# Attention and FFN on one core: a first row turned by TensorE, loads behind the row, a last tile whole

## The chip, the cores and the metric

The kernel runs on one core of a Trainium2 chip. The metric is the device time of one execution in microseconds; for the kernel before, three runs gave 1577.24, 1580.03 and 1580.16, median 1580.03. The engines are TensorE (PE), VectorE (DVE), ScalarE (ACT), GpSimd (POOL) and SyncE (SP, which here only issues DMAs).

## The reference

Eight batches of eight heads, sequence 1152, head size 64. The queries are averaged in pairs, so 576 of them meet 1152 keys; the result feeds an FFN over 4608 tokens whose activation is h - tanh(h).

```
q_pool = q.reshape(B, H, S // factor, factor, D).mean(axis=3)
scores = scale * np.matmul(q_pool, k.transpose(0, 1, 3, 2))
scores = scores - np.max(scores, axis=-1, keepdims=True)
attn = np.exp(scores)
attn = attn / (np.sum(attn, axis=-1, keepdims=True) + 1e-09)
return np.matmul(attn, v)
...
h = x @ w_in
g = h - np.tanh(h)
return g @ w_out
```

## The kernel before

**Pairs of heads.** The attention works on 32 pairs; a pair is two heads of one batch, one on the lower and one on the upper 64 partitions. A tile `raw` (128 partitions) holds 576 columns of summed queries and 1152 columns of keys. `kq_h` is it rounded to the short float that TensorE takes at full rate, `kq_l` the rest, so that a product is three matmuls: high-high, high-low, low-high.

**A pair's course on PE.** 18 places of scores (two halves of the queries by nine key tiles). Each place has the three kinds of product and a fourth matmul, `ps<-m_row,sel`, that adds the negative row maximum from a row tile `m_row`; ScalarE then takes the exponential into `p`. Then come 18 places of p times v, and last `sums`, 24 records of `ps<-sum,ones` that add what POOL had summed over three key tiles each (`add_p`, twelve POOL additions a pair). Between a pair's score places stand the 14 `max_part` of the next pair: a product in high parts alone, and a DVE reduce into `mx`. `max_row` then makes the row: reduces into `nm`, a DVE transpose into `tr`, a DMA out to `m_dram` and one or two back into `m_row`.

**What sets the order.** Every engine runs its instructions in the order of the program, through one helper, so nearly all instructions bear its line (L37). Work beside the main course is put at a place of a pair by `add(pair, place, function)`; places 0 to 17 are scores, NS + 0 to NS + 17 (NS = 18) are p times v. SP's DMAs all go out on one queue, in order. `load(pi)` issues q and k of a pair three pairs ahead, at place 10. POOL issues two accumulating DMAs at a pair's end: `kq_l<-raw` (NS + 16) and, by `query_sums`, `raw<-in_q_dram` (NS + 17), which adds the other query of each two to the one that `load` brought. Every fourth pair ends a batch: `fetch_sums` and `reciprocals` bring the sums of its heads (`s_dram`, `rec`, `r_dram`).

**Weights.** From pair 2 on, 16 blocks of raw weights (8-byte numbers) are loaded (`w_raw`, `w_off`, 1 MB each), taken apart on ScalarE and DVE in six steps (begin, clamp, mid, high, a mask, low; four steps a pair), and stored (`wi_dram`, `wo_dram`, 512 KB twice). Late pairs also prepare the first x tile (`x_l`, `x_r`, `x_h`), and in pair 27 `first_weights` loads the first FFN weights.

**The start.** Pair 0's q comes whole, its k in three parts. Nine `max_part` give the first three query tiles, and a first `max_row` their part of the row; the other five parts and a second `max_row` follow.

**The FFN.** 9 chunks of 512 tokens by 16 feature tiles. A step is `hidden` (12 matmuls), `shrink` (ScalarE: square, two polynomials' squares, tanh; POOL: a mask; DVE: five operations and a masked copy) and `second` (12 matmuls into four `ps_o`). `g_high` and `g_low` part the result in two. Only the very last step is cut in halves of 256 tokens (`parts`): its first half gives the first two of its four output tiles, and they are stored before the second half's.

Of the kernel before, what the change touches and what calls it, by code (L numbers as in the profile page):

```python
# [6 lines left out]

F32 = mybir.dt.float32
# [4 lines left out]
ALU = mybir.AluOpType  # L13
# [33 lines left out]
def attention_ffn_kernel(  # L47
# [50 lines left out]
    chunks = [(t, 512) for t in range(0, NTOK, 512)]  # L98
    wi, wo = {}, {}

    def load_w(tile_, f, which):

        t = tile_[:, which * 1024:(which + 1) * 1024] if tile_.shape[1] == 2048 else tile_[:, 0:1024]
        sp.dma_start(t.bitcast(F32), (wi_dram, wo_dram)[which][f].rearrange("p s n -> p (s n)" if which else "p s c n -> p (s c n)"))
        if which == 0:
            wi[f] = t.rearrange("p (s c n) -> p s c n", s=2, c=NP)
        else:
            wo[f] = t.rearrange("p (s n) -> p s n", s=2)

    class X:  # L110
# [25 lines left out]
        def high(self, c):  # L136
            act.activation(self.h[:, c], self.r[c], AF.Copy)
# [27 lines left out]
    def hidden(s):  # L165

        mm = [(w, x, c) for w, x in ((0, s.x.h), (0, s.x.l), (1, s.x.h)) for c in range(NP)]
        for k in s.parts:
            for j, (w, x, c) in enumerate(mm):
                pe.matmul(s.h[:, k], wi[s.f][:, w, c], x[:, c, k], start=(j == 0), stop=(j == len(mm) - 1))  # L170

    def g_high(s, k=slice(0, 512)):
        act.activation(s.g_h[:, k], s.s1[:, k], AF.Copy)

    def g_low(s, k=slice(0, 512)):
        pool.tensor_tensor(s.g_l[:, k], s.s1[:, k], s.g_h[:, k].bitcast(F32), op=ALU.subtract)

    def shrink(s, before):
        t = lambda name, dt=F32: gp.tile([P, 512], dt, name=name)
        all_ = t("g_u"), t("g_t"), t("g_s1"), t("g_s2"), t("g_m", mybir.dt.uint8), s.w  # L180
        s.s1 = all_[2]
        s.g_h = gp.tile([P, 512], F32R, name="g_hi", bufs=LAG + 1)
        s.g_l = gp.tile([P, 512], F32R, name="g_lo", bufs=LAG + 1)
        for k in s.parts:
            shrink_part(s, before, s.h[:, k], *(a[:, k] for a in all_))
            before = None

    def shrink_part(s, before, h, u, th, s1, s2, m, w):
        act.activation(u, h, AF.Square)
        act.activation(s1, u, AF.Square, bias=pc[:, 0:1])  # L190
        act.activation(s2, u, AF.Square, bias=pc[:, 1:2])
        act.activation(th, h, AF.Tanh)
        if before:
            g_high(before)
        pool.tensor_scalar(m, u, T_POLY * T_POLY, None, op0=ALU.is_ge)
        if before:
            g_low(before)
        dve.scalar_tensor_tensor(w, u, -P0, h, op0=ALU.add, op1=ALU.mult)
        dve.scalar_tensor_tensor(w, u, PL, w, op0=ALU.mult, op1=ALU.mult)
        dve.scalar_tensor_tensor(w, s1, P1, w, op0=ALU.add, op1=ALU.mult)  # L200
        dve.scalar_tensor_tensor(s1, s2, P2, w, op0=ALU.add, op1=ALU.mult)
        dve.tensor_tensor(th, h, th, op=ALU.subtract)
        dve.copy_predicated(s1, m, th)

    def second(s, js):
        po = s.chunk.po
        for j in js:
            if len(po) <= j:
                po.append(ps_o.tile([P, DM], F32, name="ps_o"))
            ts = slice(j * P, (j + 1) * P)  # L210
            for i, (g, w) in enumerate(((s.g_h, 0), (s.g_h, 1), (s.g_l, 0))):
                pe.matmul(po[j], g[:, ts], wo[s.f][:, w], start=(s.f == 0 and i == 0), stop=(s.f == NF - 1 and i == 2))

    def store(c, j):
        o = outp[0].tile([P, DM], F32, name="o_f")
# [13 lines left out]
    with ExitStack() as actx:  # L229
# [9 lines left out]

        ones = st.tile([P, 64], F32, name="ones")[:, 0:32]  # L240
        nc.vector.memset(ones, 1.0)
        sel = st.tile([P, P], F32R, name="sel")
        nc.gpsimd.memset(sel.bitcast(F32), 0.0)
        m_row = [st.tile([P, 5 * P], F32R, name=f"m_row{i}") for i in range(2)]
# [12 lines left out]
        def psum():  # L257
            return ring.tile([P, 2, 512], F32, name="ps")
# [9 lines left out]

        pairs = {}

        def load(pi, ks=1):

            w = pairs[pi] = Pair()
            w.b, w.hp = divmod(pi, NP)
            w.raw = rawp.tile([P, KQ], F32, name="raw")
            if pi < 2:
                w.q2 = qp.tile([P, 2, SQ], F32, name="q2")
            if pi != 1:
                sp.dma_start(w.raw[:, 0:SQ] if pi else w.q2, q[w.b, w.hp][:, 0] if pi else q[w.b, w.hp])
            for a in range(0, S, S // ks):  # L280
                sp.dma_start(w.raw[:, SQ + a:SQ + a + S // ks], k[w.b, w.hp][:, a:a + S // ks])
            if pi == 1:
                sp.dma_start(w.q2, q[w.b, w.hp])

        def query_sums(pi, eng=dve):

            w = pairs[pi]
            if pi < 2:
                eng.tensor_tensor(w.raw[:, 0:SQ], w.q2[:, 0], w.q2[:, 1], op=ALU.add)
            else:  # L290
                pool.dma_start(w.raw[:, 0:SQ], q[w.b, w.hp][:, 1], accum_op=ALU.add, max_dma_last_dim=4 * KQ)
            w.mx = sm.tile([P, 32], F32, name="mx")[:, 0:30].rearrange("p (t c h) -> p t c h", t=5, h=2)
# [49 lines left out]
        def max_row(pi, ta=0, tb=4):  # L342
# [15 lines left out]
            if tb == 4:  # L358
                sp.dma_start(to[:, 4 * P:SQ].rearrange("h (j n) -> h j n", n=32),
                             by[2, nt - 1].rearrange("(h j) n -> h j n", h=2))  # L360

        def scores(w, half, kt):

            ks = slice(SQ + kt * P, SQ + (kt + 1) * P)
            qs = slice(half * HQ, (half + 1) * HQ)
            ps = psum()
            mm = [(w.hi[:, ks], w.hi[:, qs]), (w.hi[:, ks], w.lo[:, qs]), (w.lo[:, ks], w.hi[:, qs]), (sel, w.m[:, qs])]
            for i, (a, b) in enumerate(mm):
                for h in range(2):
                    pe.matmul(ps[:, h, 0:HQ], rows(a, h), rows(b, h), start=(i == 0), stop=(i == 3), skip_group_check=True)  # L370
            p = ppool.tile([P, 2, HQ], F32, name=f"p{kt}")
            act.activation(p, ps[:, :, 0:HQ], AF.Exp, scale=1.0 / 16)
            return p
# [31 lines left out]

        WN = 1024
        lo_b, hi_b = 2.0 ** -15, float.fromhex("0x1.dffffep+16")

        class W:
            def __init__(self, kind, i, c):
# [16 lines left out]
            def steps(self, then):  # L429
                ts, stt = dve.tensor_scalar, dve.scalar_tensor_tensor  # L430

                def f(x):
                    return x.bitcast(F32)

                def begin():
                    self.t = wp.tile([P, WN], I32, name="w_t")
                    act.activation(f(self.t), f(self.raw)[:, :, 1], AF.Abs)

                def mid():
                    self.hl = wp.tile([P, 2, WN], I32, name="w_hl")  # L440
# [1 line left out]

                def clamp():
                    ts(f(self.t), f(self.t), lo_b, hi_b, op0=ALU.max, op1=ALU.min)
                    ts(self.t, self.t, 0x08000000, 3, op0=ALU.bitwise_xor, op1=ALU.logical_shift_left)
                    ts(self.t, self.t, 0x7FFFFFFF, None, op0=ALU.bitwise_and)

                def high():
                    stt(self.hl[:, 0], self.hw, -0x80000000, self.t, op0=ALU.bitwise_and, op1=ALU.bitwise_or)
# [38 lines left out]
        def add(pi, place, f, *args):  # L488
            at.setdefault((pi, place), []).append(lambda: f(*args))

        for pi in range(1, n_pair):
            for i in range(12):
                add(pi - 1, (0, 3, 5, 7, 9, 11, 13, 14, 15, 17, 17, 17)[i], max_part, pi, i)
            for i in range(12, 14):
                add(*((pi - 2, 2 * NS - 1) if pi > 1 else (0, NS - 1)), max_part, pi, i)
            add(pi - 1, NS - 1, max_row, pi)
        add(1, 5, blocks[0].load)
        for pi in range(n_pair):
            if pi >= 2:
                add(max(pi - 3, 0), 10 if pi > 2 else 0, load, pi)  # L500
                add(pi - 2, NS, high, pi)
                add(pi - 2, NS + 9, minus_high, pi)
                add(pi - 2, NS + 16, low, pi)
                add(max(pi - 3, 0), NS + 17 if pi > 2 else 8, query_sums, pi)
            if pi >= 1:
                add(pi - 1, 2, load_v, pi)
            if pi % NP == NP - 1 and pi < n_pair - 1:
                add(pi + 1, 10, fetch_sums, pi // NP)
                add(pi + 1, NS + 10, reciprocals, pi // NP)
# [21 lines left out]
            add(n_pair - (2 if i > 3 else 5), NS + 3 + 2 * i, first_weights, *a)  # L531

        act.activation(ones[0:1, 0:1], ones[0:1, 0:1], AF.Exp, scale=0.0)
        load(0, 3)
        load(1)
        load_v(0)
        query_sums(0)
        high(0, ((0, SQ), (SQ, SQ + CH), (SQ + CH, SQ + 2 * CH), (SQ + 2 * CH, KQ)))
        low(0, ((0, SQ), (SQ, KQ)))
        query_sums(1, pool)  # L540
        for i in range(9):
            max_part(0, i)
        max_row(0, 0, 3)
        for i in range(9, 14):
            max_part(0, i)
        max_row(0, 3, 4)
        high(1)
        minus_high(1)
        add(0, 6, low, 1)

# [96 lines left out]
    second(a, range(4))  # L647
    for i, k in enumerate(b.parts):
        g_high(b, k)
        g_low(b, k)  # L650
        for j in range(2 * i, 2 * i + 2):
            second(b, [j])
            store(b.chunk, j)


# [36 lines left out]
```

## Time and profile before

| | |
|---|---|
| median of three runs | 1580.03 us |
| time of the profiled execution | 1580.02 us |
| its span | 1578.3 us |
| DMA | 193.59 MB, 88676 packets |
| ordinary pair, between two row sums | 23.85 us |

The profile is of one execution. The span runs from the first instruction to the last; the time has 1.7 us around it. Attention lies between 5 and 800 us, the FFN behind. A timeline row gives start and duration of a group of like instructions, and in brackets how long the engine stood idle before it and what ended that.

### The profile page before, as it was taken

How to read it: one execution, taken by the hardware profiler on the slowest of the kernel's cores; microseconds unless marked ns; L12 is line 12 of the kernel's file. 1: busy time of each engine (PE TensorE's matmuls, PEld its weight loads, DVE VectorE, ACT ScalarE, POOL GpSimd, SP SyncE). 2: the span in 40 equal slices, each digit the busy share in tenths (PEclk: the TensorE clock that was granted, in tenths of full speed). 3: DMA queues.
4: the chain of work that ended last, by engine and by line, in shares of the span. 5: the costliest groups of instructions: out<-in, count | busy, mean ns of one | idle time of the engine just before them, and what ended most of it. 6: DMA issues, size and time to landing. Idle time of an engine off the chain costs nothing.

```text
span 1578.3 us, 30802 instructions
## 1 busy us (share of the span) xinstructions
PE 1556.5 (99%) x12012; PEld 1224.1 (78%) x12012; DVE 1185.8 (75%) x1558; ACT 978.3 (62%) x1617; POOL 1155.3 (73%) x813
## 2 busy tenths in 40 slices
PE   7999999999999999999999999999999999999998
PEld 5777777777777777676778888888888888888886
DVE  6588787888888887765457777777777777777776
ACT  5667667667667667675645655565555555565654
POOL 6788888898888897785857576666767575766664
PEclk9999999999999999999999999999999999999999
DMA  5757767768677769573171201010010101020000
GB/s 169 207 177 218 222 185 220 218 211 252 186 237 210 218 201 267 143 231 91 63 285 70 68 15 67 14 61 14 13 61 14 67 14 67 14 67 14 28 1 27
DMA packets 88676, 193.59 MB, mean 123 GB/s; under 512 B 12882, under 2 KB 39890, under 8 KB 86482
## 3 DMA queue, kind: packets, MB, share of 16 engines
q1 hardware_dynamic: 79746, 155.35, 27.4%
q0 software_dynamic: 8784, 36.28, 12.7%
q8 instruction: 94, 1.54, 0.4%
q14 instruction: 52, 0.43, 0.1%
HBM read 126.12 MB, written 38.04 MB: 104 GB/s over the span
## 4 chain that ended last, share of the span: by engine, by line
PE 91%; DMA 3%; ACT 2%; DVE 2%; issue 1%; SPq 0%; POOLq 0%; POOL 0%; ACTq 0%; DVEq 0%
PE ps L37 43%; PE ps_o L37 24%; PE ps_h L37 24%; ACT p L37 2%; DMA s_dram<-s_s 2%; DVE mx L37 1%; DMA m_row<-m_dram 0%; DMA x_r<-r_dram 0%; DMA m_dram<-tr 0%; DVE w_hl L37 0%; SPq L37 0%; DVE w_t L37 0%; DMA q<-in_q_dram 0%; DVE ps_w L37 0%; DVE x_r L37 0%
## 5 line engine op out<-in xcount | busy, mean ns | idle before, releaser
L37 DVE TENSOR_REDUCE mx<-ps 128x2 f32<-128x768 f32 x448 | 400.1, 924 | 145.2 <-PE ps L37 145.0
L37 POOL TENSOR_SCALAR g_m<-g_u 128x512 uint8<-128x512 f32 (+1 forms) x145 | 247.2, 1705 | 184.6 <-ACT g_u L37 170.3
L37 POOL TENSOR_TENSOR sum<-p,p 128x576 f32<-128x576 f32 x192 | 294.4, 1533 | 117.9 <-ACT p L37 117.9
L37 ACT ACTIVATE p<-ps 128x576 f32<-128x576 f32 x576 | 347.3, 653 | 48.0 <-PE ps L37 27.6
L37 POOL TENSOR_TENSOR sum<-sum,p 128x576 f32<-128x576 f32 x192 | 291.7, 1519 | 15.0
L37 PE MATMUL ps<-p,v 128*64 128x288 f32 x2304 | 286.4, 407 | 3.5 <-DVE mx L37 0.4
L37 PE MATMUL ps<-kq_h 64*128 64x288 f32 (+1 forms) x1920 | 273.4, 338 | 8.4 <-ACT kq_h L37 6.4
L37 PEld LDWEIGHTS ps<-p,v 128*64 128x64 f32 x2304 | 162.5, 137 | 119.6 <-ACT p L37 10.2
L37 POOL TENSOR_TENSOR g_lo<-g_s,g_hi 128x512 fp32r<-128x512 f32 (+1 forms) x145 | 186.9, 1289 | 87.4 <-ACT g_hi L37 87.4
L37 PE MATMUL ps_o<-w,g_hi 128*128 128x512 f32 x792 | 244.0, 389 | 1.0 <-ACT g_hi L37 1.0
L37 ACT ACTIVATE g_u<-ps_h 128x512 f32<-128x512 f32 (+1 forms) x142 | 84.0, 591 | 217.8 <-PE ps_h L37 216.3
L37 PEld LDWEIGHTS ps<-kq_h 64*128 64x128 f32 x1920 | 179.1, 186 | 49.6 <-issue 13.9
L37 DVE SCALAR_TENSOR_TENSOR ps_w<-g_u,ps_h 128x512 f32<-128x512 f32 (+1 forms) x142 | 98.4, 693 | 153.2 <-ACT g_t L37 153.2
L37 PE MATMUL ps_h<-x_h,w 128*128 128x512 f32 (+1 forms) x800 | 212.0, 387 | 0.1
L37 ACT ACTIVATE g_s<-g_u,pc 128x512 f32<-128x512 f32 x290 | 193.4, 715 | 11.4 <-POOL g_lo L37 0.2
L37 PE MATMUL ps<-m_row,sel 64*128 64x288 f32 x1152 | 171.4, 293 | 2.8 <-DMA m_row<-m_dram 2.2
L37 PEld LDWEIGHTS ps_o<-w,g_hi 128*128 128x128 f32 x792 | 148.5, 188 | 32.1 <-ACT g_hi L37 1.4
L37 PEld LDWEIGHTS ps_h<-x_h,w 128*128 128x128 f32 x800 | 149.3, 188 | 31.1 <-DVE g_t L37 0.5
L37 PE MATMUL ps<-kq_l,kq_h 64*128 64x288 f32 x1152 | 171.7, 293 | 0.0
L37 PE MATMUL ps<-kq_h,kq_l 64*128 64x288 f32 x1152 | 171.6, 293 | 0.0
L37 PE MATMUL ps_o<-w,g_lo 128*128 128x512 f32 x396 | 154.4, 390 | 0.1
L37 DVE COPY_PREDICATED g_s<-g_m,g_t 128x512 f32<-128x512 uint8 (+1 forms) x145 | 110.5, 762 | 17.0 <-POOL g_m L37 2.1
(114 smaller groups left out, 2379.7 us busy)
## 6 DMA issues: line engine op xcount, KB each, us to landing
kq_l<-raw POOLq DMA_DIRECT2D x31, 864.0 KB, 8.0
v<-in_v_dram SPq DMA_DIRECT2D x32, 576.0 KB
raw<-in_k_dram SPq DMA_DIRECT2D x31, 576.0 KB
x_dram<-o_s SPq DMA_DIRECT2D x32, 288.0 KB
x_l<-x_dram SPq DMA_DIRECT2D x9, 1024.0 KB
out_dram<-o_f SPq DMA_DIRECT2D x36, 256.0 KB
raw<-in_q_dram SPq DMA_DIRECT2D x30, 288.0 KB
raw<-in_q_dram POOLq DMA_DIRECT2D x30, 288.0 KB, 10.0
```

Source lines behind the costliest of these rows:

```text
L37: i = f(*args, **kwargs)
```

## The change

Four parts.

1. **Pair 0.** q comes in two parts (256 and 320 columns) and k in three, in the order q, k, q, k, k; DVE sums and ScalarE rounds in the same pieces. The maximum parts run by key part first (0, 3, 6, 1, ...). The maxima of the first three query tiles go into a zeroed tile `nz` (a `w_hl` buffer) and are turned by six matmuls against an identity `eye` (a `w_t` buffer, made on POOL), from where ScalarE copies 384 columns into `m_row`. The parts 12 and 13 and the second `max_row`, which still goes through DRAM, move to places 0 and 1 of pair 0.
2. **Loads.** `load(pi)` moves from place 10 to NS + 5, which on SP is behind the row's DMAs.
3. **Weights.** The clamp has two DVE operations instead of three.
4. **The last feature tile.** `hidden`, ScalarE's four operations and the mask run whole; DVE's part stays in halves. The second half's `g_low` runs on DVE, and PE takes both outputs' high products ahead of the low ones.

```diff
-        for k in s.parts:
-            for j, (w, x, c) in enumerate(mm):
-                pe.matmul(s.h[:, k], wi[s.f][:, w, c], x[:, c, k], start=(j == 0), stop=(j == len(mm) - 1))
+        for j, (w, x, c) in enumerate(mm):
+            pe.matmul(s.h, wi[s.f][:, w, c], x[:, c], start=(j == 0), stop=(j == len(mm) - 1))
...
+        u, th, s1, s2, m, _ = all_
+        act.activation(u, s.h, AF.Square)
         act.activation(s1, u, AF.Square, bias=pc[:, 0:1])
         act.activation(s2, u, AF.Square, bias=pc[:, 1:2])
-        act.activation(th, h, AF.Tanh)
+        act.activation(th, s.h, AF.Tanh)
...
+        for k in s.parts:
+            shrink_part(s.h[:, k], *(a[:, k] for a in all_))
...
+        eye = wp.tile([P, WN], F32, name="w_t")[:, 0:P]
+        nz = wp.tile([P, 2, WN], F32, name="w_hl")[:, 0, 0:6 * 64].rearrange("p (t h n) -> p t h n", t=3, h=2)
+        nc.vector.memset(nz, 0.0)
+        make_identity(nc, eye)
...
+        QA = 2 * P
+        FIRST = [(0, QA), (SQ, SQ + CH), (QA, SQ), (SQ + CH, SQ + 2 * CH), (SQ + 2 * CH, KQ)]
...
+        def max_row_pe(w):
+
+            w.m = m_row[0]
+            ps = psum()
+            for t in range(3):
+                for h in range(2):
+                    tiled(ps[:, 0, t * P:(t + 1) * P], nz[:, t, h], eye, h, start=True, stop=True)
+            act.activation(w.m[:, 0:3 * P], ps[:, 0, 0:3 * P], AF.Copy)
...
                 def clamp():
                     ts(f(self.t), f(self.t), lo_b, hi_b, op0=ALU.max, op1=ALU.min)
-                    ts(self.t, self.t, 0x08000000, 3, op0=ALU.bitwise_xor, op1=ALU.logical_shift_left)
-                    ts(self.t, self.t, 0x7FFFFFFF, None, op0=ALU.bitwise_and)
+                    ts(self.t, self.t, 4, 1, op0=ALU.logical_shift_left, op1=ALU.logical_shift_right)
...
+        for i in (12, 13):
+            add(0, i - 12, max_part, 0, i)
+        add(0, 1, max_row, 0, 3, 4)
         for pi in range(1, n_pair):
             for i in range(12):
-                add(pi - 1, (0, 3, 5, 7, 9, 11, 13, 14, 15, 17, 17, 17)[i], max_part, pi, i)
+                add(pi - 1, (0 if pi > 1 else 2, 3, 5, 7, 9, 11, 13, 14, 15, 17, 17, 17)[i], max_part, pi, i)
...
-                add(max(pi - 3, 0), 10 if pi > 2 else 0, load, pi)
+                add(max(pi - 3, 0), NS + 5 if pi > 2 else 0, load, pi)
...
-        load(0, 3)
+        load(0)
         load(1)
         load_v(0)
-        query_sums(0)
-        high(0, ((0, SQ), (SQ, SQ + CH), (SQ + CH, SQ + 2 * CH), (SQ + 2 * CH, KQ)))
+        query_sums(0, parts=((0, QA), (QA, SQ)))
+        high(0, FIRST)
         low(0, ((0, SQ), (SQ, KQ)))
         query_sums(1, pool)
-        for i in range(9):
+        for i in (0, 3, 6, 1, 4, 7, 2, 5, 8):
             max_part(0, i)
-        max_row(0, 0, 3)
-        for i in range(9, 14):
+        dve.tensor_reduce(nz[:, :, :, 0], pairs[0].mx[:, 0:3].rearrange("p t c h -> p t h c"), axis=AX.X, op=ALU.max, negate=True)
+        for i in (9, 10):
             max_part(0, i)
-        max_row(0, 3, 4)
         high(1)
+        max_row_pe(pairs[0])
+        max_part(0, 11)
...
     for i, k in enumerate(b.parts):
         g_high(b, k)
-        g_low(b, k)
-        for j in range(2 * i, 2 * i + 2):
-            second(b, [j])
+        g_low(b, k, dve if i else pool)
+        js = range(2 * i, 2 * i + 2)
+        if i:
+            second(b, js, (0, 1))
+        for j in js:
+            second(b, [j], (2,) if i else (0, 1, 2))
             store(b.chunk, j)
```

SP's queue in pair 4, an ordinary pair in which a block of raw weights is loaded: from the last DMA of the batch's sums to the next pair's output. `raw` is the tile that `load` fills, `tr` the row of maxima; before:

```order
L37 DMA rec<-s_dram 128x36
L37 DMA raw<-in_q_dram 128x576
L37 DMA raw<-in_k_dram 128x1152
L37 DMA m_dram<-tr 128x128
L37 DMA m_row_122<-m_dram 2x16x32
L37 DMA m_row_122<-m_dram 2x2x32
L37 DMA w_raw<-in_w_in_dram 128x4096
L37 DMA w_off<-in_w_in_dram 128x4096
L37 DMA wi_dram<-w_hl 128x8x128 x2
L37 DMA r_dram<-rec 128x36
L37 DMA x_dram<-o_s 128x576
```

and after:

```order
L38 DMA rec<-s_dram 128x36
L38 DMA m_dram<-tr 128x128
L38 DMA m_row_129<-m_dram 2x16x32
L38 DMA m_row_129<-m_dram 2x2x32
L38 DMA w_raw<-in_w_in_dram 128x4096
L38 DMA w_off<-in_w_in_dram 128x4096
L38 DMA raw<-in_q_dram 128x576
L38 DMA raw<-in_k_dram 128x1152
L38 DMA wi_dram<-w_hl 128x8x128 x2
L38 DMA r_dram<-rec 128x36
L38 DMA x_dram<-o_s 128x576
```

The row's three DMAs now come first, and q and k stand behind both weight loads; the stores come behind them.

SP's queue from pair 27, where the first FFN weights are loaded, to the row of pair 29; before:

```order
L37 DMA w_hl<-wi_dram 128x1024
L37 DMA w_hl<-wo_dram 128x1024
L37 DMA w_t<-wi_dram 128x1024
L37 DMA x_dram<-o_s 128x576
L37 DMA s_dram<-s_s 4x288
L37 DMA v<-in_v_dram 128x1152
L37 DMA rec<-s_dram 128x36
L37 DMA raw<-in_q_dram 128x576
L37 DMA raw<-in_k_dram 128x1152
L37 DMA m_dram<-tr 128x128
L37 DMA m_row_122<-m_dram 2x16x32
L37 DMA m_row_122<-m_dram 2x2x32
```

and after:

```order
L38 DMA raw<-in_q_dram 128x576
L38 DMA raw<-in_k_dram 128x1152
L38 DMA w_off<-wi_dram 128x1024
L38 DMA w_off<-wo_dram 128x1024
L38 DMA w_hl<-wi_dram 128x1024
L38 DMA w_hl<-wo_dram 128x1024
L38 DMA w_t<-wi_dram 128x1024
L38 DMA x_dram<-o_s 128x576
L38 DMA s_dram<-s_s 4x288
L38 DMA v<-in_v_dram 128x1152
L38 DMA rec<-s_dram 128x36
L38 DMA m_dram<-tr 128x128
```

One load of q and k moved in among the first weights, and the next no longer stands between `rec` and the write of the row.

PE's first instructions, pair 0's maxima and its first score places, where `w_t` is the identity and `w_hl` holds the maxima; before:

```order
L37 MATMUL ps<-kq_h 128x384 x24
L37 MATMUL ps<-kq_h,q_last_125 128x384 x3
L37 MATMUL ps<-kq_h 128x288 x2
L37 MATMUL ps<-kq_l,kq_h 128x288 x2
L37 MATMUL ps<-kq_h,kq_l 128x288 x2
L37 MATMUL ps<-m_row_121,sel 128x288 x2
```

and after:

```order
L38 MATMUL ps<-kq_h 128x384 x22
L38 MATMUL ps<-w_t,w_hl 64x128 x6
L38 MATMUL ps<-kq_h 128x384 x2
L38 MATMUL ps<-kq_h 128x288 x2
L38 MATMUL ps<-kq_l,kq_h 128x288 x2
L38 MATMUL ps<-kq_h,kq_l 128x288 x2
L38 MATMUL ps<-m_row_128,sel 128x288 x2
L38 MATMUL ps<-kq_h,q_last_132 128x384 x2
```

Six turning matmuls came in behind 11 parts, and the three q_last products moved behind the first score place.

More of the change, by code (lines that the diff above doesn't have):

```diff
@@ L5 @@
 from concourse import mybir
+from concourse.masks import make_identity
 from concourse._compat import with_exitstack
@@ L99, in attention_ffn_kernel @@
     wi, wo = {}, {}
+    WN = 1024
     def load_w(tile_, f, which):
@@ L167, in hidden, with g_low @@
         mm = [(w, x, c) for w, x in ((0, s.x.h), (0, s.x.l), (1, s.x.h)) for c in range(NP)]
-        for k in s.parts:
-            for j, (w, x, c) in enumerate(mm):
-                pe.matmul(s.h[:, k], wi[s.f][:, w, c], x[:, c, k], start=(j == 0), stop=(j == len(mm) - 1))
+        for j, (w, x, c) in enumerate(mm):
+            pe.matmul(s.h, wi[s.f][:, w, c], x[:, c], start=(j == 0), stop=(j == len(mm) - 1))
     def g_high(s, k=slice(0, 512)):
         act.activation(s.g_h[:, k], s.s1[:, k], AF.Copy)
-    def g_low(s, k=slice(0, 512)):
-        pool.tensor_tensor(s.g_l[:, k], s.s1[:, k], s.g_h[:, k].bitcast(F32), op=ALU.subtract)
+    def g_low(s, k=slice(0, 512), eng=pool):
+        eng.tensor_tensor(s.g_l[:, k], s.s1[:, k], s.g_h[:, k].bitcast(F32), op=ALU.subtract)
     def shrink(s, before):
@@ L183, in shrink @@
         s.g_l = gp.tile([P, 512], F32R, name="g_lo", bufs=LAG + 1)
[L184 to L189, printed above, removed]
+        u, th, s1, s2, m, _ = all_
+        act.activation(u, s.h, AF.Square)
         act.activation(s1, u, AF.Square, bias=pc[:, 0:1])
         act.activation(s2, u, AF.Square, bias=pc[:, 1:2])
-        act.activation(th, h, AF.Tanh)
+        act.activation(th, s.h, AF.Tanh)
         if before:
@@ L197, in shrink_part @@
             g_low(before)
+        for k in s.parts:
+            shrink_part(s.h[:, k], *(a[:, k] for a in all_))
+    def shrink_part(h, u, th, s1, s2, m, w):
         dve.scalar_tensor_tensor(w, u, -P0, h, op0=ALU.add, op1=ALU.mult)
@@ L203, in shrink_part, with second @@
         dve.copy_predicated(s1, m, th)
-    def second(s, js):
+    def second(s, js, which=(0, 1, 2)):
         po = s.chunk.po
@@ L210, in second @@
             ts = slice(j * P, (j + 1) * P)
-            for i, (g, w) in enumerate(((s.g_h, 0), (s.g_h, 1), (s.g_l, 0))):
-                pe.matmul(po[j], g[:, ts], wo[s.f][:, w], start=(s.f == 0 and i == 0), stop=(s.f == NF - 1 and i == 2))
+            for i in which:
+                pe.matmul(po[j], (s.g_h, s.g_h, s.g_l)[i][:, ts], wo[s.f][:, i % 2], start=(s.f == 0 and i == 0),
+                          stop=(s.f == NF - 1 and i == 2))
     def store(c, j):
@@ L269, in attention_ffn_kernel, with load @@
         pairs = {}
-        def load(pi, ks=1):
+        QA = 2 * P
+        FIRST = [(0, QA), (SQ, SQ + CH), (QA, SQ), (SQ + CH, SQ + 2 * CH), (SQ + 2 * CH, KQ)]
+        def load(pi):
             w = pairs[pi] = Pair()
@@ L277, in load, with query_sums @@
                 w.q2 = qp.tile([P, 2, SQ], F32, name="q2")
[L278 to L285, printed above, removed]
+            for a, b in FIRST if pi == 0 else ((SQ, KQ), (0, SQ)) if pi == 1 else ((0, SQ), (SQ, KQ)):
+                if a >= SQ:
+                    sp.dma_start(w.raw[:, a:b], k[w.b, w.hp][:, a - SQ:b - SQ])
+                elif pi < 2:
+                    sp.dma_start(w.q2[:, :, a:b], q[w.b, w.hp][:, :, a:b])
+                else:
+                    sp.dma_start(w.raw[:, a:b], q[w.b, w.hp][:, 0])
+        def query_sums(pi, eng=dve, parts=((0, SQ),)):
             w = pairs[pi]
             if pi < 2:
-                eng.tensor_tensor(w.raw[:, 0:SQ], w.q2[:, 0], w.q2[:, 1], op=ALU.add)
+                for a, b in parts:
+                    eng.tensor_tensor(w.raw[:, a:b], w.q2[:, 0, a:b], w.q2[:, 1, a:b], op=ALU.add)
             else:
@@ L404, in sums @@
             sp.dma_start(s_dram[w.b, w.hp].rearrange("h (a n) -> (h a) n", a=2), s[0:P:32])
-        WN = 1024
-        lo_b, hi_b = 2.0 ** -15, float.fromhex("0x1.dffffep+16")
+        lo_b, hi_b = 2.0, float.fromhex("0x1.dffffep+32")
         class W:
@@ L436, in begin @@
                     self.t = wp.tile([P, WN], I32, name="w_t")
-                    act.activation(f(self.t), f(self.raw)[:, :, 1], AF.Abs)
+                    act.activation(f(self.t), f(self.raw)[:, :, 1], AF.Abs, scale=2.0 ** 16)
                 def mid():
```

## The prediction

> **What bounds the kernel now.** I read the busy times first, then what TensorE waited for, then the busy times by stretches, and after that the timelines of the few places where TensorE is not full.
>
> ```profile
> PE 1556.5 (99%) x12012; PEld 1224.1 (78%) x12012; DVE 1185.8 (75%) x1558; ACT 978.3 (62%) x1617; POOL 1155.3 (73%) x813
> ...
> L37 PE MATMUL ps<-m_row,sel 64*128 64x288 f32 x1152 | 171.4, 293 | 2.8 <-DMA m_row<-m_dram 2.2
> ```
> ```profile
> PE ps L37 <- ACT kq_h L37: 6.4, 1, 6.4
> ```
> ```profile
> 46.00:570.00 524.00, 521.52 (x5864) 391.37 (x5862) 429.30 (x482) 358.38 (x563) 444.93 (x308) 1.00 0.72 212
> ...
> 750.00:1540.00 790.00, 789.32 (x3761) 649.29 (x3758) 579.03 (x840) 458.63 (x792) 525.33 (x364) 1.00 0.14 51
> ```
>
> TensorE (PE) is busy 99% of the span. In the rows by stretches the columns are length, then busy time of PE, weight loads, DVE, ACT, POOL, then granted clock: PE lacks 2.5 us in 524, and 0.7 in 790. The change adds and removes next to no matmul, so what can be won lies in the first 46 us, between 570 and 750, and behind 1540. What can be lost is larger: any new wait in a full pair of heads goes straight into the time. VectorE's (DVE) sixteen removed weight operations, for example, are worth nothing by themselves: DVE has idle time in every stretch and PE hardly waits.
>
> My sum starts from the profiled execution: span 1578.3, time 1580.0 us; the median of the runs is the same 1580.03.
>
> **The start.** Rows of DVE, PE and SP, start and duration in us:
>
> ```profile
> 4.48 0.76 DVE L37 TENSOR_TENSOR raw<-q 128x576 f32<-128x576 f32 x1 [3.09 <-DMA q<-in_q_dram]
> 7.16 7.87 DVE L37 TENSOR_REDUCE mx<-ps 128x2 f32<-128x768 f32 x9 [1.92 <-PE ps L37]
> ```
> ```profile
> 6.43 1.84 PE L37 MATMUL ps<-kq_h 64*128 64x384 f32 x8 [6.43 <-ACT kq_h L37]
> ...
> 19.09 0.61 PE L37 MATMUL ps<-m_row,sel 64*128 64x288 f32 x2 [0.60 <-DVE mx L37]
> ...
> 21.97 0.35 PE L37 MATMUL ps<-kq_l,kq_h 64*128 64x288 f32 x2
> ```
> ```profile
> 15.66 0.33 SPq L37 DMA_DIRECT2D m_dram<-tr  x1
> 17.22 0.65 SPq L37 DMA_DIRECT2D m_row<-m_dram  x1
> ```
>
> Nine reduces run back to back (0.874 each) from 7.16 to 15.03, and the row that comes of them reaches PE at 19.09. Part one is the q load: its first part has 256 of 576 columns, so DVE's sum costs 0.34 instead of 0.76, ScalarE's first piece shrinks in the same proportion (estimate 0.3 less), and 44% of the bytes land before 4.48; by how much is not shown, between 0 and 2.5 us, and I take 0.8, near the low end since a fixed latency stays. The first reduce moves from 7.16 to about 5.7, the ninth ends at 13.5.
>
> Part two is the row. Now it costs 4.06 us from 15.03 to 19.09, of which the write out and the read back through DRAM are 3.4. After: a small reduce (0.3), six transposing matmuls, a ScalarE copy of 384 columns (0.5, from the 0.65 that 512 columns take below). The matmuls are not in this trace; the nearest row is the group of row sums below, also full-precision against a constant, 24 records in 1.66. Bounds are 0.2 (by columns) and 3.3 (the whole group at half the clock); I take 1.3. The row would be there at 15.9. PE then still has one maximum part and the first place's own products, so I put the subtraction at about 17.4: 1.7 earlier. Three q_last matmuls (0.5) now come later, and the slow clock that lasts until 21.97 ends sooner (0.8). Together **-2.0** (bounds -2.4 and 0). The identity that POOL builds is wanted at 13.8 and has 7 us of loads to hide behind; if it came late, each us would count whole. Nought is reached where the second part of the row, still through DRAM and with pair 2's loads now ahead of it on SP, lands after the ninth place wants it: by my count it lands at 24.1 and is wanted at 24.3.
>
> **Pair 29.** The chain of waits, then PE (`[idle <- releaser]` last):
>
> ```profile
> 692.31 13.49 DMA s_dram<-s_s
> ...
> 706.24 0.37 SPq L37
> ...
> 706.67 0.50 SPq L37
> ...
> 707.26 4.39 DMA m_dram<-tr
> ...
> 711.67 6.70 DMA m_row<-m_dram
> ```
> ```profile
> 718.40 0.61 PE L37 MATMUL ps<-m_row,sel 64*128 64x288 f32 x2 [2.17 <-DMA m_row<-m_dram]
> ...
> 719.37 0.44 PE L37 MATMUL ps<-kq_l,kq_h 64*128 64x288 f32 x2
> ```
> ```profile
> 690.14 1.66 PE L37 MATMUL ps<-sum,ones 128*32 128x288 f32 x24
> ...
> 713.99 1.66 PE L37 MATMUL ps<-sum,ones 128*32 128x288 f32 x24
> ...
> 732.22 1.19 PE L37 MATMUL ps<-x_h,w_raw 128*128 128x512 f32 x4
> ...
> 735.16 2.16 PE L37 MATMUL ps<-p,v 128*64 128x288 f32 x16
> ...
> 744.77 1.66 PE L37 MATMUL ps<-sum,ones 128*32 128x288 f32 x24
> ```
>
> Row sums stand at the end of each pair: 690.14 to 713.99 is an ordinary pair, 23.85. The next takes 30.78, of which 2.94 are the first FFN matmuls (732.22 to 735.16): 3.99 are lost. The row's write stood on SP behind the loads of q and k, and its bytes behind theirs (0.86 MB), and the read back then met POOL's accumulating transfer. The change puts q and k behind the row: the write goes out at about 707.1 with nothing ahead, takes near the 1.56 of the start instead of 4.39, and the read lands about 711.5, wanted at 716.2. So **-4.0**. The other bound is 0: load 30 now stands among the first weights, ahead of the 13.49 us transfer, which then ends some 2 us later, and the row would land just as POOL's data begin to move.
>
> The wait is 2.17, the loss 3.99; the rest is clock, since for 3.5 us two matmuls side by side take 0.44 where they else take 0.293. The Trainium skill, "TensorE: Matmul & The Clock Gate", Part 1, has the clock fall only after a whole idle window of about 3.4 us; by it this stall would cost 2.17, and its removal bring 2.2 instead of 4.0. The trace disagrees: a gap of 2.17 was enough.
>
> **Pairs 24 and 25.**
>
> ```profile
> 592.61 1.66 PE L37 MATMUL ps<-sum,ones 128*32 128x288 f32 x24
> ...
> 616.90 1.66 PE L37 MATMUL ps<-sum,ones 128*32 128x288 f32 x24 [0.38 <-ACT o_s L37]
> ...
> 641.83 1.66 PE L37 MATMUL ps<-sum,ones 128*32 128x288 f32 x24
> ```
> ```profile
> 614.50 1.30 DVE L37 TENSOR_TENSOR x_r<-x_l,x_r 128x512 f32<-128x512 f32 x1 [2.01 <-DMA x_r<-r_dram]
> ```
> ```profile
> 608.82 1.14 SPq L37 DMA_DIRECT2D x_r<-r_dram  x2
> ```
>
> These two pairs take 24.29 and 24.93, 0.44 and 1.08 above 23.85. DVE stood 2.01 us for x_r, whose read went out behind the loads of q and k; everything that DVE then does is late. With the loads behind, x_r is there 2 us earlier, and a weight step is gone. **-1.5**, bounds -0.5 (only the step) and -1.6.
>
> **The tail.** ScalarE (ACT):
>
> ```profile
> 1570.55 1.29 ACT L37 ACTIVATE o_f<-ps_o 128x512 f32<-128x512 f32 x2 [1.41 <-PE ps_o L37]
> 1571.74 0.41 ACT L37 ACTIVATE g_hi<-g_s 128x256 fp32r<-128x256 f32 x1
> ```
>
> With the last tile whole on ScalarE, DVE's second half no longer waits for it and ends about 1.1 us sooner. But the second g_hi stands on ScalarE behind two output copies that wait for PE, and runs the moment they end (1571.84). So only what PE gains counts: 12 matmuls for 24, some 0.25. **-0.3**, bounds 0 and -0.7. The third product on DVE instead of POOL lies beside PE's other products.
>
> **What the later loads cost.** In seven pairs (4, 7, ... 22) q and k now go out right behind 2 MB of raw weights, and POOL's accumulate of the other half of q waits for q. Behind that accumulate on POOL stand the next pair's twelve sums. Pair 4, with SP, POOL, the queues' packets and megabytes from 138 to 143 and from 144 to 145, and PE:
>
> ```profile
> 135.04 0.33 SPq L37 DMA_DIRECT2D w_raw<-in_w_in_dram  x1
> ```
> ```profile
> 138.63 1.19 POOL L37 DMA_DIRECT2D raw<-in_q_dram  x1
> 142.90 1.43 POOL L37 TENSOR_TENSOR sum<-p,p 128x576 f32<-128x576 f32 x1 [3.08 <-ACT p L37]
> ...
> 159.68 1.73 POOL L37 TENSOR_TENSOR sum<-sum,p 128x576 f32<-128x576 f32 x1
> ```
> ```profile
> q1 hardware_dynamic: 244, 1.62, 97.0%
> q0 software_dynamic: 1, 0.01, 0.7%
> ```
> ```profile
> q0 software_dynamic: 28, 0.19, 93.5%
> q1 hardware_dynamic: 37, 0.02, 8.4%
> ```
> ```profile
> 162.83 1.66 PE L37 MATMUL ps<-sum,ones 128*32 128x288 f32 x24
> ```
>
> POOL is done at 161.41; PE wants the last sum two thirds into its group, about 163.85, so 2.4 us are free. Until 143 the weights fill the hardware queue and POOL's kq_l, issued at 138, moves one packet. If what SP has queued goes first, q's 0.29 MB follow at 0.33 MB/us and land about 144.5 (0.6 of it for the completion, an estimate from the 1.56 that the small row write takes in all), the accumulate is issued until 145.6 (1.19), and the sums start 2.7 late instead of at 142.90. Against 2.4, and a quarter microsecond that POOL wins since a DVE weight step less runs beside it, that is a wait of 0.05 to 0.6 in each of seven pairs. I take 0.3: **+2.0**, bounds 0 and (below) 20. In the other pairs the loads stand behind at most 1 MB of stores and land before POOL's first sum. The accumulate itself lands later too, still before ScalarE's kq_h wants it.
>
> **Sum:** -2.0 - 4.0 - 1.5 - 0.3 + 2.0 = -5.8, so 1580.0 - 5.8 = **1574.2 us**, own range 1571.5 to 1576.8.
>
> **The rivals.**
>
> *A, the loads wait in turn.* Once both queues have work, one packet of each goes: from 144 to 145 there are 28 of POOL's and 37 of SP's. If q's 128 rows are 128 packets and go like that, they need 3.5 us from 143 on, q lands near 147, the sums start 5.3 late, and 2.9 per pair is lost: 7 x 2.9 = +20. With half of q through before kq_l starts it is 1.3, +9. The point from which it decides is q landing behind some 144.5; then every us costs seven. With the gains (-7.8) that gives 1581 to 1592, in the middle 1586.5: slower. For it speaks that 1:1 row, against it that kq_l stood still until the weights were through. The Trainium skill, "DMA: Bandwidth & Descriptors", section "Queues, rings and completion order", has each engine go round robin between its queues, packet by packet. By that rule alone the loads would share and this rival holds; the row of 1.62 MB against one packet does not look like taking turns.
>
> *B, partial gains.* The seven pairs cost 0.8 each (+5.6), or pair 29's row lands on POOL's data again (+4.0): 1577.8 or 1578.2, within 0.2%.
>
> *C, the start gives nothing*, its second row part being late (PE would show a wait for the row at the ninth place): 1576.2.
>
> **How the numbers follow.** A measurement of this kernel can tell about 0.2%, 3.2 us, so faster means below 1576.9 and slower above 1583.2. The forecast has 0.43, C 0.04: faster 0.47. B has 0.23. A has 0.30, of which 0.06 end below 1583.2 and some 0.10 above 1588: same 0.29, slower 0.24. Of the forecast's share I leave 0.06 below 1571.5 (full gains, no cost). The range is 1571.5 to 1588.
>
> **What would show it.** In the changed kernel's profile: the first subtraction at about 17.4 with no m_dram ahead of it; pair 29 without a wait for the row and 26.8 between its row sums; no DVE wait for x_r near 614; in the pair behind pair 4, POOL's first sum released by its own accumulate rather than by ScalarE, near 143, and PE's row sums waiting for POOL by 0.3. I am wrong if these waits are above 1 us, or if row writes elsewhere now meet the loads.

## The result, and the profile after

The changed kernel takes 1622.98 us (median of 6 runs, 1620.21 to 1629.29), the kernel before beside it 1578.78: a ratio of 1.029, interval 1.0265 to 1.0314. It is 44 us slower, forecast was 1574.2. The profiled execution is the longest of the six: its span is 1627.5 us, 49.2 above that of before.

Its page, first the busy times, then the chain that ended last by engine:

```profile
PE 1579.2 (97%) x12012; PEld 1236.6 (76%) x12012; DVE 1184.3 (73%) x1544; ACT 978.6 (60%) x1615; POOL 1152.5 (71%) x813
...
PE 79%; POOL 9%; DMA 5%; DVE 4%; ACT 2%; issue 1%; SPq 0%; ACTq 0%; POOLq 0%; DVEq 0%
```

POOL is 9% of the chain, and was not on it before:

```profile
PE 91%; DMA 3%; ACT 2%; DVE 2%; issue 1%; SPq 0%; POOLq 0%; POOL 0%; ACTq 0%; DVEq 0%
```

What PE waited for in the changed kernel (us in total, times, longest):

```profile
PE ps L38 <- POOL sum L38: 29.8, 16, 2.4
PE ps L38 <- ACT kq_h L38: 6.5, 2, 5.3
PE ps L38 <- DVE w_hl L38: 1.3, 1, 1.3
```

and what POOL waited for:

```profile
POOL raw L38 <- DMA raw<-in_q_dram: 89.0, 18, 11.7
```

So the wait named as the deciding one was the right one, and far longer than forecast. The timeline of SP and of POOL in pair 4, the first of the seven in which raw weights go out ahead of q and k (start, duration, idle before and its releaser):

```profile
137.38 0.33 SPq L38 DMA_DIRECT2D w_raw<-in_w_in_dram  x1
137.76 0.42 SPq L38 DMA_DIRECT2D w_off<-in_w_in_dram  x1
138.28 0.38 SPq L38 DMA_DIRECT2D raw<-in_q_dram  x1
```
```profile
140.39 0.87 POOL L38 DMA_DIRECT2D kq_l<-raw  x1
152.13 0.87 POOL L38 DMA_DIRECT2D raw<-in_q_dram  x1 [10.87 <-DMA raw<-in_q_dram]
152.69 1.76 POOL L38 TENSOR_TENSOR sum<-p,p 128x576 f32<-128x576 f32 x1
...
164.35 2.26 POOL L38 TENSOR_TENSOR sum<-sum,p 128x576 f32<-128x576 f32 x1
...
170.88 1.40 POOL L38 TENSOR_TENSOR sum<-sum,p 128x576 f32<-128x576 f32 x1
```

q goes out at 138.28, and POOL stands idle for 10.87 us until q has landed and it can issue the accumulate; the twelve sums behind it start at 152.69 and end at 172.28. The queues' packets, megabytes and share of the DMA engines, from 139 to 144 and from 145 to 151:

```profile
q1 hardware_dynamic: 227, 1.73, 95.9%
```
```profile
q0 software_dynamic: 135, 0.88, 70.7%
q1 hardware_dynamic: 222, 0.61, 29.5%
```

(q1 is SP's queue, q0 POOL's.) In the first five microseconds the weights have the DMA engines to themselves, POOL's queue moving nothing. Then kq_l runs (0.88 MB), and SP's queue, with q and k in it, gets 0.61 MB in six microseconds. That is 0.10 MB/us, less than a third of the 0.35 that it had alone (1.73 MB in five). On PE:

```profile
165.18 0.67 PE L38 MATMUL ps<-sum,ones 128*32 128x288 f32 x2
166.66 0.69 PE L38 MATMUL ps<-sum,ones 128*32 128x288 f32 x8 [0.81 <-POOL sum L38]
169.49 1.19 PE L38 MATMUL ps<-sum,ones 128*32 128x288 f32 x8 [2.14 <-POOL sum L38]
172.33 1.18 PE L38 MATMUL ps<-sum,ones 128*32 128x288 f32 x6 [1.65 <-POOL sum L38]
173.44 0.61 PE L38 MATMUL ps<-kq_h 64*128 64x288 f32 x2
...
176.31 0.29 PE L38 MATMUL ps<-kq_h,kq_l 64*128 64x288 f32 x2
```

The row sums, 1.66 us in an ordinary pair, last from 165.18 to 173.44, which is 6.6 too long; PE then runs on the slow clock until 176.3 (the granted clock is 0.50 from 173.5 to 176.0 and 1.00 from 176.4 on), which is some 1.3 more. From the end of pair 4's row sums to that of pair 24's the profile of before takes 477.9 us and this one 530.0: the seven stalls cost 52.1. Pair 29 gives 3.9 back, the first pair ends 2.3 later than before, and small differences of -1.3 make it 49.2.

### The profile page after: what moved, and what is told of

Read it like the earlier page. It is cut to its first block, busy times and chain, and to the rows that moved or that the text cites. A ratio compares the mean times of both kernels' runs of the same rounds, so it can differ in the third digit from the quotient of the medians.

```text
span 1627.5 us, 30768 instructions
## 1 busy us (share of the span) xinstructions
PE 1579.2 (97%) x12012; PEld 1236.6 (76%) x12012; DVE 1184.3 (73%) x1544; ACT 978.6 (60%) x1615; POOL 1152.5 (71%) x813
## 4 chain that ended last, share of the span: by engine, by line
PE 79%; POOL 9%; DMA 5%; DVE 4%; ACT 2%; issue 1%; SPq 0%; ACTq 0%; POOLq 0%; DVEq 0%
PE ps L38 32%; PE ps_o L38 24%; PE ps_h L38 23%; POOL sum L38 8%; DMA raw<-in_q_dram 4%; DVE mx L38 2%; DVE w_hl L38 1%; ACT p L38 1%; SPq L38 0%; DMA q<-in_q_dram 0%; DVE x_r L38 0%; DVE w_t L38 0%; POOL g_lo L38 0%; DVE nm L38 0%; ACT kq_l L38 0%
## 5 line engine op out<-in xcount | busy, mean ns | idle before, releaser
L38 POOL TENSOR_SCALAR g_m<-g_u 128x512 uint8<-128x512 f32 x144 | 245.9, 1708 | 184.0 <-ACT g_u L38 169.6
L38 POOL TENSOR_TENSOR sum<-p,p 128x576 f32<-128x576 f32 x192 | 298.1, 1553 | 63.2 <-ACT p L38 63.2
L38 PE MATMUL ps<-kq_h 64*128 64x288 f32 (+1 forms) x1920 | 278.2, 343 | 7.7 <-ACT kq_h L38 6.5
L38 PEld LDWEIGHTS ps<-p,v 128*64 128x64 f32 x2304 | 162.6, 137 | 119.6 <-ACT p L38 10.2
L38 POOL TENSOR_TENSOR g_lo<-g_s,g_hi 128x512 fp32r<-128x512 f32 x144 | 185.9, 1291 | 86.5 <-ACT g_hi L38 86.5
L38 PEld LDWEIGHTS ps<-kq_h 64*128 64x128 f32 x1920 | 182.6, 191 | 51.7 <-issue 18.4
L38 ACT ACTIVATE g_u<-ps_h 128x512 f32<-128x512 f32 x141 | 83.9, 595 | 216.4 <-PE ps_h L38 216.4
L38 PE MATMUL ps_h<-x_h,w 128*128 128x512 f32 x792 | 211.8, 389 | 0.1
```

The source lines that it names most:

```text
L38: i = f(*args, **kwargs)
```

## The experiments

Each run is set against the kernel before as it ran beside it, on the same chip: median 1577.07 (e1 to e4), 1580.18 (e5 to e8), 1577.11 (e9, e10, e12, e13). Ratios are to that median, with a 95% interval.

**e1, the loads back at place 10.**

```diff
-                add(max(pi - 3, 0), NS + 5 if pi > 2 else 0, load, pi)
+                add(max(pi - 3, 0), 10 if pi > 2 else 0, load, pi)
```

> The changed kernel with the loads of q and k back at place 10, all else as changed. Theory T1 (nearly all of the loss is POOL waiting for q in the seven pairs that load raw weights): POOL's waits for raw<-in_q_dram, 89 us in all in the changed kernel, fall below 10, PE's waits for POOL sums (29.8) fall to 0, and the time comes back to 1577 to 1582 (the stall of pair 29 is there again, the start is some 2 us longer). Rival T2 (a good part of the loss comes from the other edits, the start, the clamp or the tail): 1590 or more.

1579.01, ratio 1.0008 (0.9995 to 1.0021). PE has no wait for POOL sums left. T1 holds: of the 44 us nothing that could be told lies in the start, the clamp or the tail.

**e2, the loads alone.** The kernel before with the one line above, the other way.

> The kernel before with the loads of q and k at NS + 5, nothing else. T1: the whole loss and the gain of pair 29 are here: 1616 to 1626 (7 pairs at 6 to 8 us, less 4 to 5). T2: well under that, 1580 to 1605, since the other edits are missing.

1628.46, ratio 1.0327 (1.030 to 1.0354): the whole loss, just above the range of T1. Its median is 5 us above the changed kernel's, but the two were not run side by side, the intervals of their ratios overlap, and the changed kernel's own runs reach 1629.29. Whether the other edits win anything back while POOL is the bound is not shown.

**e3, the loads behind the row but ahead of the weights.**

```diff
-                add(max(pi - 3, 0), NS + 5 if pi > 2 else 0, load, pi)
+                add(max(pi - 3, 0), NS if pi > 2 else 0, load, pi)
```

> The changed kernel with the loads at NS, so behind the row but ahead of the raw weights on SP. T1 in the form that the place behind 2 MB of weights is what delays q: no PE wait for POOL sums, no wait for the row in pair 29, 1573 to 1579. Rival T3 (any load of q and k behind the row comes too late for POOL's accumulate, with or without weights): PE still waits for POOL in many pairs, above 1590.

1575.18, ratio 0.9982 (0.9971 to 0.9994). The loads go out five places earlier in the program, and the loss becomes a small gain. T3 falls: the row may go first, and q still comes in time. PE's timeline, the row sums of pairs 23 to 29:

```profile
592.37 1.66 PE L38 MATMUL ps<-sum,ones 128*32 128x288 f32 x24
616.22 1.66 PE L38 MATMUL ps<-sum,ones 128*32 128x288 f32 x24
640.60 1.66 PE L38 MATMUL ps<-sum,ones 128*32 128x288 f32 x24
...
712.74 1.66 PE L38 MATMUL ps<-sum,ones 128*32 128x288 f32 x24
739.59 1.66 PE L38 MATMUL ps<-sum,ones 128*32 128x288 f32 x24
```

Pair 29 takes 26.85 here instead of 30.78, pair 24 23.85 instead of 24.29, pair 25 24.38 instead of 24.93.

**e4, q's accumulate ahead of kq_l's on POOL.**

```diff
-                add(pi - 2, NS + 16, low, pi)
-                add(max(pi - 3, 0), NS + 17 if pi > 2 else 8, query_sums, pi)
+                add(pi - 2, NS + 17, low, pi)
+                add(max(pi - 3, 0), NS + 16 if pi > 2 else 8, query_sums, pi)
```

> The changed kernel with POOL's two accumulating transfers swapped: the one of q first, kq_l behind it, so that kq_l's packets can't run beside q's. Theory T4 (q waits its turn packet by packet beside kq_l): q lands as soon as the weights are through, POOL's waits for q fall from some 10 us in each of the seven pairs to 4 to 6, PE's waits for POOL to under 1 us a pair, time 1577 to 1590. Rival T5 (q is late by its place behind 2 MB of weights alone): POOL's waits stay at 9 to 11 us, and with kq_l's issue also behind them the time is 1622 to 1632.

1593.37, ratio 1.0096 (1.0075 to 1.0117): 30 us of the 44 are gone, though the range was missed by 3. POOL's waits for q in the seven pairs are 5.6 to 8.5 us, not 4 to 6, and PE's for POOL 1.4 a pair, not under 1. SP and POOL in pair 4:

```profile
136.45 0.33 SPq L38 DMA_DIRECT2D w_raw<-in_w_in_dram  x1
136.83 0.42 SPq L38 DMA_DIRECT2D w_off<-in_w_in_dram  x1
137.35 0.38 SPq L38 DMA_DIRECT2D raw<-in_q_dram  x1
```
```profile
146.67 0.88 POOL L38 DMA_DIRECT2D raw<-in_q_dram  x1 [7.17 <-DMA raw<-in_q_dram]
147.27 1.18 POOL L38 DMA_DIRECT2D kq_l<-raw  x1
147.83 2.06 POOL L38 TENSOR_TENSOR sum<-p,p 128x576 f32<-128x576 f32 x1
```

The accumulate goes out 10.2 us behind the weights' issue (136.45 to 146.67), in the changed kernel 14.75 (137.38 to 152.13). The difference, 4.5 us, is what kq_l beside q costs. The rest is the place behind 2 MB, which by itself still leaves PE 9.8 us of waits for POOL in all. T4 and T5 each hold for a part; T5 alone is out.

**e8, the weights one step later.** `then.load()` moves from `high` to the mask behind it.

> The changed kernel (loads at NS + 5) with each block of raw weights loaded one step later, so that in pairs 4, 7, 10 and on the weights stand behind q and k, while in other pairs (6, 9 and on) the next block now comes ahead of q and k. Theory (order behind 2 MB of weights): the long POOL waits for q leave pairs 4, 7, ... and turn up in the others, 8 to 12 us each, total 1615 to 1640. Rival (something else in pairs 4, 7, ... makes q late, such as the batch's sums or POOL's own state): the stalls stay in those pairs.

1621.08, ratio 1.0256 (1.0239 to 1.0274). In pair 4 the wait is gone:

```profile
147.53 1.19 POOL L38 DMA_DIRECT2D raw<-in_q_dram  x1
```

and in pairs 3, 6, 9 and on POOL now waits 3.5 to 4.8 us, not 8 to 12. That the total lies in the range is no support: this kernel has a new wait. ScalarE now stands for the weights themselves:

```profile
ACT w_t L38 <- DMA w_raw<-in_w_in_dram: 36.7, 4, 9.6
ACT w_t L38 <- DMA w_raw<-in_w_out_dram: 33.8, 4, 8.7
```

So it shows that the stall leaves pair 4 with the order, and on the total it is inconclusive.

**e12, only q ahead of the weights.** q's load at NS, k's left at NS + 5.

> The changed kernel with only q's load moved ahead of the raw weights (NS), k's still behind them (NS + 5). Theory: POOL waits for q alone, and k has until ScalarE's kq_h some 18 us later: no POOL stall in pairs 4, 7, ..., 1574 to 1578 beside a kernel before of 1577 to 1580. Rival: k late behind weights and kq_l holds up ScalarE's kq_h and kq_l, or POOL's accumulate still lands late beside them: above 1585.

1574.21, ratio 0.9979 (0.997 to 0.9988). SP and POOL in pair 4:

```profile
135.05 0.33 SPq L38 DMA_DIRECT2D raw<-in_q_dram  x1
135.48 0.38 SPq L38 DMA_DIRECT2D w_raw<-in_w_in_dram  x1
135.91 0.42 SPq L38 DMA_DIRECT2D w_off<-in_w_in_dram  x1
136.39 0.42 SPq L38 DMA_DIRECT2D raw<-in_k_dram  x1
```
```profile
138.86 1.19 POOL L38 DMA_DIRECT2D raw<-in_q_dram  x1
143.13 1.44 POOL L38 TENSOR_TENSOR sum<-p,p 128x576 f32<-128x576 f32 x1 [3.09 <-ACT p L38]
```

k, twice as large, still stands behind 2 MB and beside kq_l, and it costs nothing. The whole loss hangs on 288 KB that POOL, with twelve sums behind it in its order, waits for.

**e5 and e6, the start.** e5 has the new start alone on the kernel before; e6 is e3 with the old start.

```diff
-        load(0)
+        load(0, 3)
...
-        query_sums(0, parts=((0, QA), (QA, SQ)))
-        high(0, FIRST)
+        query_sums(0)
+        high(0, ((0, SQ), (SQ, SQ + CH), (SQ + CH, SQ + 2 * CH), (SQ + 2 * CH, KQ)))
```

> The kernel before with the new start of pair 0 alone (q in two parts, the first row turned by TensorE), loads at place 10, old clamp and tail. My forecast gave the start -2.0. Theory S1, from the traces: the first subtraction comes 1.2 to 1.5 us sooner, three products come later and the slow clock ends at a time that varies by some 5 us from run to run whatever the start: -1 to +1 us, no difference that can be told. Rival S2 (the new start keeps PE on the slow clock longer, as in the changed kernel's trace): +2 to +4.

> The kernel with loads at NS (ahead of the raw weights), the new clamp and the new tail, but the start of the kernel before. S1: the same as e3_loads_ahead within 1.5 us, 1574 to 1577. S2: 2 to 4 below it, 1571 to 1573.

e5: 1579.34, ratio 0.9996 (0.9983 to 1.0009). e6: 1575.86, ratio 0.9977 (0.9966 to 0.9988), beside 0.9982 of e3. S1: the new start makes no difference that can be told.

**e7, e9 and e10, the tail.** e7 is e3 with both parts' g_hi and g_lo put ahead of the output copies; e9 and e10 are e3 and e7 again, side by side.

```diff
     for i, k in enumerate(b.parts):
         g_high(b, k)
         g_low(b, k, dve if i else pool)
+    for i, k in enumerate(b.parts):
         js = range(2 * i, 2 * i + 2)
```

> e3_loads_ahead with the second half's g_hi on ScalarE ahead of the first half's output copies. Theory: the tail gains little in the changed kernel because that g_hi stands behind the two copies; put ahead, PE's 0.99 us wait for it is gone: 0.8 to 1.0 us less than e3_loads_ahead, and in the trace no idle before the last four g_hi products. Rival: DVE's second half ends as late anyway, no change of that wait.

> The same kernel as e3_loads_ahead, beside the three below on one chip: 0.2 to 0.3% under the kernel before.

> The same kernel as e7_tail_order. If the tail's order is worth what its trace shows (the last 13.2 us from the last whole g_hi become 12.0), 0.8 to 1.3 us below e9_loads_ahead_again; if not, the same.

e7: 1573.65, ratio 0.9958 (0.9944 to 0.9972). e9: 1574.90, 0.9987 (0.9978 to 0.9996). e10: 1574.03, 0.9977 (0.9969 to 0.9986). The intervals of e9 and e10 overlap, so by times alone the 0.9 between them is not settled. In the trace PE's wait is gone; the changed kernel's last four high products, and those of e10:

```profile
1621.88 1.21 PE L38 MATMUL ps_o<-w,g_hi 128*128 128x512 f32 x4 [0.99 <-ACT g_hi L38]
```
```profile
1565.83 1.09 PE L38 MATMUL ps_o<-w,g_hi 128*128 128x512 f32 x4
```

**e13, the old clamp** on e10 (with the scale and the bounds that belong to it, not shown here):

```diff
-                    ts(self.t, self.t, 4, 1, op0=ALU.logical_shift_left, op1=ALU.logical_shift_right)
+                    ts(self.t, self.t, 0x08000000, 3, op0=ALU.bitwise_xor, op1=ALU.logical_shift_left)
+                    ts(self.t, self.t, 0x7FFFFFFF, None, op0=ALU.bitwise_and)
```

> e10_tail_order_again with the old clamp, so with a VectorE weight step more in each of 16 blocks. Theory: VectorE is off the path but for pairs 24 to 26, so 0 to 1 us above e10. Rival (the longer weight work slows POOL's sums through the whole attention): 2 us or more above.

1574.61, ratio 0.998 (0.9969 to 0.9992): 0.6 above e10, inside both intervals. Where POOL is not the bound, the step is worth next to nothing.

## Why the prediction was wrong

**The step that failed** is the cost of the later loads, +2.0 in the sum, where the seven pairs cost 52 in the profile. "If what SP has queued goes first, q's 0.29 MB follow" was taken for the likely case, because kq_l had moved one packet until the weights were through. That row was read too far. It shows that kq_l waited for 2 MB, not that it would wait for what comes behind them: it starts as the weights end, and q shares with it. From 145 to 151 SP's queue gets 0.10 MB/us, where the forecast had q at 0.33. The figure for the unshared case was right: I put q at 9.5 us behind the weights' issue (144.5 against 135.04), and in e4, without sharing, the accumulate's issue at 146.67, some half a microsecond behind q, puts it near 9.7. With sharing it is 14.2 (in the chain of waits of the changed kernel q's transfer ends at 151.57).

**Rival A** named the place, the mechanism and the point from which it decides, and had 0.30. Its price was too low: 2.9 per pair and 20 in all, measured 44 in the changed kernel and 51 in e2. q landed 2.2 us later than it said (14.2 behind the weights' issue, where 147 against 135.04 is 12.0), so the sums start 7.4 late, not 5.3 (12.5 us ahead of the row sums in the changed kernel, 19.9 before). Late as they were, they ran beside VectorE's weight steps, where one takes 2.26 instead of 1.42, and the last ends 8.5 late. Less the 2.4 that were free that is 6.1, and PE lost 7.9: the broken row sums put it on the slow clock as well. I had argued in pair 29 that a stall of 2 us can cost the clock too, and did not charge it here. The high end of the range had been set by the price of one wait without those two.

**Even unshared, 0.3 per pair was too little.** e4 has lost some 18 us against e3 (1593.37 less 1575.18); by the two profiles 17.2 of it lie between the row sums of pair 4 and of pair 24, 2.5 for each of the seven pairs. Its sums also start behind kq_l's issue.

**Pair 29** was right: 26.84 between its row sums in the changed kernel and 26.85 in e3, forecast 26.8, and no wait for the row. But the profiled execution of before was not a typical one. Beside e9, most of 33 runs of before lie from 1576 to 1577.5 and six from 1578.7 to 1585; e3 and e9 have none above 1577. e1 and e5, with loads at place 10, show such waits for the row in pair 29 (2.2 and 4.0 us, the pair taking 29.31 and 33.31), e1 another of 2.1 in pair 1, and their times spread as before's do. That the stall comes in some executions only, and not always as long, fits all this, but with one profile of before it is not shown. Nor does a gap of 2.2 us always bring the slow clock, as the forecast took from the one in before. PE in e1, pair 29:

```profile
722.39 0.40 PE L38 MATMUL ps<-m_row,sel 64*128 64x288 f32 x2 [2.18 <-DMA m_row<-m_dram]
722.94 0.29 PE L38 MATMUL ps<-kq_l,kq_h 64*128 64x288 f32 x2
```

The products behind the gap take 0.29, and the pair loses 2.5 us, not 4.0. So 4.0 was the price of one execution. The gain in the median is below 4: e9 is 2.2 under before, for pair 29, pairs 24 to 25 and all else together.

**Pairs 24 and 25**: -1.0 (0.44 and 0.55, in e3) for -1.5. With the old clamp pair 25 takes 25.13, with the new one 24.39 (e13 and e10), so here the removed step is worth 0.7. VectorE's wait for x_r is gone from the changed kernel's profile, as forecast.

**The start**: 0 for -2.0. It was not rival C, since PE's list has no wait for the row. The first reduce came at 6.83, not 5.7, and the subtraction at 17.90, not 17.4. DVE, ScalarE and PE in the changed kernel:

```profile
6.42 0.49 DVE L38 TENSOR_TENSOR raw<-q 128x320 f32<-128x320 f32 x1 [2.05 <-DMA q<-in_q_dram]
6.83 7.87 DVE L38 TENSOR_REDUCE mx<-ps 128x2 f32<-128x768 f32 x9
```
```profile
15.27 1.64 ACT L38 ACTIVATE kq_h<-raw 128x1728 fp32r<-128x1728 f32 x1 [6.60 <-POOL raw L38]
16.82 0.50 ACT L38 ACTIVATE q_last<-raw 64x64 fp32r<-64x64 f32 x2
17.35 0.49 ACT L38 ACTIVATE m_row<-ps 128x384 fp32r<-128x384 f32 x1
```
```profile
15.06 1.55 PE L38 MATMUL ps<-w_t,w_hl 128*64 128x128 f32 x12 [1.34 <-DVE w_hl L38]
...
17.90 0.61 PE L38 MATMUL ps<-m_row,sel 64*128 64x288 f32 x2
...
26.30 0.29 PE L38 MATMUL ps<-kq_l,kq_h 64*128 64x288 f32 x2
```

q's second part, behind the first k, landed at 6.40; the whole q had landed at 4.46. DVE's sum of it stands ahead of the first reduce. The six turning matmuls took 1.55 (estimate 1.3), and the copy then stood on ScalarE behind pair 1's kq_h. The slow clock lasted until 26.30 instead of 21.97, where I had it end sooner; in other executions of this start it ended sooner (last section).

**The tail**: from the last whole g_hi (1565.12 of 1578.3) to the end before 13.2 us, in e9 (1561.73 of 1574.9) also 13.2. The reason given was right, the second g_hi stands behind the copies; put ahead it is 12.0 (e10: 1560.01 of 1572.0).

## What to carry to other kernels

When a load is moved back on a queue, price it by who waits for it: 576 KB of k behind the weights cost nothing, 288 KB of q 44 us, since POOL, which had twelve other instructions behind it in its order, stood for q. A row that shows one transfer waiting for another says nothing of a third that comes between them; take the shared rate as the likely case where both queues will have work. And the price of a wait in a full engine is the wait, plus what its late work collides with, and at times the clock.

## What the runs showed of the hardware

The moment at which PE's clock rises after the start differs between executions of like code. With the old start the products take 0.44 until 21.97 in the profile of before, until 23.3 in e2 and 23.8 in e6; with the new one until 20.6 in e3, 24.6 in e9, which is the same kernel on another chip, and 26.3 in the changed kernel. That is 4 us between two executions of one program. Its first pair ends at 45.11 in e3 and at 47.12 in e9, 2 us apart, as much as I had forecast for the start. The Trainium skill, "TensorE: Matmul & The Clock Gate", Part 1, says that the window which decides it runs free of the kernel, so that the moment varies; the traces agree that it varies, with more spread than its half microsecond.

From 146 to 150 in the changed kernel POOL's queue moves 105 packets and SP's 105. The Trainium skill's rule that the DMA engines take their queues in turn, packet by packet ("DMA: Bandwidth & Descriptors", "Queues, rings and completion order") is what these rows show. From 139 to 144, with kq_l issued at 140.39, they show no turns. This is no fixed delay of POOL's transfers: in pair 5 of the profile before, with nothing else under way, kq_l is issued at 161.35 and moves its first 0.10 MB from 162 to 163, beside a VectorE weight step. There it is the raw weights that wait: issued at 163.16, they move no packet until 168. Why a later transfer starts only as these earlier ones end, although the next two then take turns, was not found out.
